# The first two head groups of an mLSTM kernel worked off together instead of one after the other

## The chip, the cores and the metric

The kernel runs on one core of one Trainium2 chip. The metric is the device time in microseconds (us) of one execution, as the median of several runs; "span" is the length of one profiled execution from its first to its last instruction.

## What is computed

Three parts in a row: an mLSTM attention with a running maximum over time, a soft mixture of experts (MoE), and an MLP with a squared ReLU. Shapes: 4 batches, 8 heads, 768 steps, head size 40; 3072 tokens of 320 values behind it. Cut to what matters:

```python
def _attn_ref(q, k, v, i_gate, f_gate, o_gate):
    for t in range(S):                      # S = 768, all B*H = 32 heads at once
        m_new = maximum(f_gate[t] + m, i_gate[t])
        f_stab, i_stab = exp(f_gate[t] + m - m_new), exp(i_gate[t] - m_new)
        m = m_new
        C = f_stab * C + i_stab * einsum('bhd,bhe->bhde', v[t], k[t])
        n = f_stab * n + i_stab * k[t]
        y[t] = sigmoid(o_gate[t]) * (C @ q[t]) / maximum(abs(n @ q[t]), 1.0)

def _moe_ref(x, phi, w1, w2):               # x: tokens from y
    logits = x @ phi                        # 32 slots, softmax over tokens and over slots
    slot_out[e] = relu(slot_input[e] @ w1[e]) @ w2[e]
    return softmax(logits, 1) @ slot_out

def _moe2_ref(x, w_in, w_out):
    r = maximum(x @ w_in, 0.0)
    return (r * r) @ w_out
```

## The kernel before

The 768 steps are cut into NC = 6 chunks of 128 (L), the 32 heads into NG = 11 groups of three (the last has two). A **unit** is one chunk of one group; `units` (L417) lists the 66 units group by group: (0,0), (0,1) ... (0,5), (1,0) and so on. The order of instructions is written out by hand: each engine works off its own instructions in the order of the code, and so does the SyncE queue (SP), which issues all DMAs.

**Gate phases.** `prep(c0, c1)` (L330) turns the gates of all heads into what the units need, for chunks 0-1, 2-3 and 4-5; START (L34) names its steps by a digit for the pair of chunks and a letter: `f` and `m` are the two scans on VectorE (DVE), `i` the subtraction between them, `h` the copy of the maximum to bf16 on ScalarE (ACT), `p` the previous maximum, `a` and `b` subtractions in front of the two exponentials `A` and `B` on ACT, `r`, `u`, `l`, `v` the split of the remainder into bf16 parts (M3), `q` the transposes on TensorE (PE) that make the per-step columns `qt3`. A `G` behind a step puts it on GpSimd (POOL).

**Unit steps.** START uses capitals for the steps of a unit: `M` (e_mb, PE, three matmuls that spread M3), `E` (e_exp, ACT, three exponentials, L451), `K` (e_sel, POOL, causal mask, L458), `T` (e_st, PE, k times q, L468), `P` (e_pm, DVE, product, L480), `W` (e_wv, POOL, weighted v, L424). `D` is one step of `prep_dec` (decay factors `dec120`), `Z` the zeroing of the second group's k buffer on POOL, `~n` are n idle-filling matmuls (L197), `~~n` a second kind (L205).

**Start and loop.** All of START up to the first `|` runs ahead of the loop; each following part runs at the end of one loop pass. Pass i of the loop (L879) issues, for unit i = (g, c): loads for later groups, e_u (L493, the state update, not in the last chunk), T of unit i+2, M of unit i+3, e_uc (L509, L512) and its mask on POOL (e_mask, L528), P of unit i+2, E of unit i+3, in odd passes the products with v of the last two units (e_av, L553), e_inter (L538), K of unit i+3, and in turn the numerators (e_num). The matmul passes of fp32 operands show as two instructions.

**Fillers.** Work of other stages is handed out in small steps by `filler` and `advance`: the tanh of the output gate (sigm, L651), the finish of a group (fin: POOL products L613, DVE L622), the MoE logits of a batch (moe_tokens, L668, L674; each third waits for the groups that it reads), and the narrowing of w_in (win_all, loads at L168, ACT L140 and L144, DVE L148 and L152).

**Buffers.** Group g uses `par[g % 2]` for k (block-diagonal, zeroed once), q, and the token-major v and k; so the loads of group g+2 wait for the last readers of group g.

Of the kernel before, what the change touches and what calls it, by code (L numbers as in the profile page):

```python
# [33 lines left out]
START = "~42 1f 1i 1m 1h 1p 1b 1B 1aG 1r 2f 1u 1A 1v 1q 1l M0 2iG E0 M1 K0 W T0 T1 2m E1 K1 3f 2p 2b 2a ~24 2h 3i 3m 2B Z0 2r 2A 2v 2u P0 3p 3bG D0 3h Z1 ~3 2q ~~5 2l M2 E2 D0 P1 3a 3A 3B K2 D0 D0 3r 3u D0 | 3l 3v 3q | D1 D1 | D1 D1 D1 |"  # L34
# [8 lines left out]
def kernel(  # L43
# [155 lines left out]
    def warm64(n):  # L199
        t = bank("m")  # L200
        for w in (128, 41):
            for _ in range(n):
                for o, r in ((dum, 0), (t, 64)):
                    a = ident[r : r + 40]
                    nc.tensor.matmul(o[:, 0:w], lhsT=a, rhs=a[:, 0:w], start=True, stop=True)  # L205

# [111 lines left out]
    nc.vector.tensor_reduce(out=gmask, in_=gj, axis=AX.X, op=ALU.add)  # L318
    nc.vector.tensor_reduce(out=gs3, in_=gj.rearrange("p g j -> p j g"), axis=AX.X, op=ALU.add)
    nc.vector.tensor_copy(hsel, gs3.unsqueeze(2).to_broadcast([32, 3, D]))  # L320
    nc.vector.tensor_copy(sel4, selF.unsqueeze(1).to_broadcast([128, 4, 32]))
# [523 lines left out]
    def start_exp(c):  # L845
        e_mb(0, c)
        e_exp(0, c)
        e_sel(0, c)
# [30 lines left out]
    for i, (g, c) in enumerate(units):  # L879
        if c == NC - 2 and 0 < g + 2 < NG:  # L880
            load_kb(g + 2)
        if i == 0:
            load_kb(1)
        if c == 0 and g + 1 < NG:
            load_q(g + 1)
        if c == 1 and g + 1 < NG:
            load_kv(g + 1)
        if i == 0:
# [62 lines left out]
        if i in (0, 2):  # L951
            e_wv(0, i + 2, i + 4)
        elif i > 2 and i + 3 < NU and units[i + 3][1] % 3 == 0:
            e_wv(units[i + 3][0], units[i + 3][1], units[i + 3][1] + 3)
# [525 lines left out]
```

## Time and profile before

| | us |
|---|---|
| median of 3 runs | 397.05 (396.72 to 397.13) |
| the profiled execution, whole | 396.4 |
| its span | 394.7 |
| PE busy in the span | 381.7 (97%) |
| DVE / ACT / POOL busy | 264.8 / 251.9 / 103.3 |
| the loop's first e_u starts | 17.39 |

The profiled execution has 1.7 us around its span and lies 0.65 us under the median. Engines run side by side, so busy times do not add up. PE's busy time includes modelled ends of pipelined matmuls, so that a busy PE can still have waited; the chain of work that ended last tells where it did.

### The profile page before, as it was taken

Reading aid. Unit: us, or ns where it says so; the run is one execution under the profiler, and the core shown is the slowest. Engines: PE = TensorE matmul, PEld = TensorE weight load, DVE = VectorE, ACT = ScalarE, POOL = GpSimd, SP = SyncE. Lnnn points to the kernel's source line nnn. Section 1 sums busy time; section 2 is a strip of 40 time slices with the busy share of each in tenths; the row PEclk is TensorE's granted clock in tenths of the full one; section 3 lists DMA queues with packets and bytes.
Section 4 is the critical chain, followed back from the end, with each engine's and each line's share of the span. In section 5 each row is a group of like instructions: output and inputs, shape, how many; then the busy total and the mean of one; then the engine's idle time right before and its main releaser. Section 6 shows DMA issues by size and latency. Waiting matters only on the chain.

```text
span 394.7 us, 9282 instructions
## 1 busy us (share of the span) xinstructions
PE 381.7 (97%) x3497; PEld 337.2 (85%) x3497; DVE 264.8 (67%) x612; ACT 251.9 (64%) x575; POOL 103.3 (26%) x208
## 2 busy tenths in 40 slices
PE   7998999999999999999998999999999999999996
PEld 5888889889888885434688999999999999999996
DVE  8857788887988686546699856555655655655551
ACT  3677665677667752345598776676666667667662
POOL 6565676767667646100000000000000000000000
PEclk9999999999999999999999999999999999999999
DMA  6588578799879789899100020010001002001001
GB/s 203 168 264 281 181 211 275 244 343 351 268 276 315 213 320 321 284 330 424 48 1 2 0 69 1 2 66 2 1 17 51 2 0 68 0 2 67 2 0 66
DMA packets 18665, 56.62 MB, mean 143 GB/s; under 512 B 2357, under 2 KB 6181, under 8 KB 18237
## 3 DMA queue, kind: packets, MB, share of 16 engines
q1 hardware_dynamic: 18621, 56.04, 41.7%
q8 instruction: 27, 0.44, 0.5%
q14 instruction: 17, 0.14, 0.1%
HBM read 52.10 MB, written 3.93 MB: 142 GB/s over the span
## 4 chain that ended last, share of the span: by engine, by line
PE 79%; DMA 5%; ACT 3%; POOL 2%; DVE 2%; issue 2%; SPq 0%; DVEq 0%; ACTq 0%; POOLq 0%
PE ps_mb L1378 17%; PE ps_st L1378 15%; PE ps_lt L1378 8%; PE ps_st L468 8%; PE ps_o L553 5%; PE ps_o L538 4%; PE ps_o L1302 4%; DMA ring<-in_w_dram 3%; PE ps_st L493 3%; PE ps_mb L437 2%; PE ps_m L668 2%; PE ps_m L1302 2%; PE ps_lt L674 2%; DMA stage<-in_w_in_dram 1%; PE ps_st L1098 1%
## 5 line engine op out<-in xcount | busy, mean ns | idle before, releaser
L1325 DVE CAST hi<-ring 128x512 fp32r<-128x512 f32 x91 | 38.8, 426 | 60.7 <-ACT ring L1324 50.7
L1326 DVE TENSOR_TENSOR lo<-ring,hi 128x512 fp32r<-128x512 f32 x96 | 66.5, 693 | 10.0
L451 ACT ACTIVATE w<-ps_mb,qt 128x128 f32<-128x128 f32 x192 | 56.7, 370 | 22.9 <-PE ps_mb L437 18.7
L1307 ACT ACTIVATE ring<-ps_o 128x512 f32<-128x512 f32 x65 | 38.9, 598 | 36.6 <-PE ps_o L1302 36.5
L1324 ACT ACTIVATE ring<-ring 128x512 f32<-128x512 f32 x91 | 57.5, 632 | 2.9
L468 PE MATMUL ps_st<-par 120*128 120x128 f32 (+1 forms) x384 | 54.0, 276 | 0.0
L1378 PE MATMUL ps_mb<-wohlh,hi 128*128 128x320 f32 x160 | 49.6, 311 | 0.0
L1378 PE MATMUL ps_mb<-wohlh,lo 128*128 128x320 f32 x160 | 49.5, 310 | 0.0
L1378 PE MATMUL ps_mb<-wohll,hi 128*128 128x320 f32 x160 | 49.3, 309 | 0.0
L468 PEld LDWEIGHTS ps_st<-par 120*128 120x128 f32 (+1 forms) x384 | 47.9, 191 | 0.5 <-issue 0.5
L458 POOL TENSOR_SCALAR_AFFINE_SELECT w<-w 128x384 f32<-128x384 f32 (+1 forms) x66 | 36.8, 559 | 37.4 <-ACT w L451 28.7
L1378 PE MATMUL ps_st<-wohlh,hi 128*128 128x320 f32 x144 | 44.8, 311 | 0.0
L1378 PE MATMUL ps_st<-wohlh,lo 128*128 128x320 f32 x144 | 44.7, 310 | 0.0
L1378 PE MATMUL ps_st<-wohll,hi 128*128 128x320 f32 x144 | 44.6, 310 | 0.0
L480 DVE TENSOR_TENSOR p<-ps_st,w 128x384 f32<-128x384 f32 (+1 forms) x66 | 35.5, 538 | 4.9 <-POOL w L458 3.8
L1378 PEld LDWEIGHTS ps_mb<-wohll,hi 128*128 128x128 f32 x160 | 30.1, 188 | 1.3
L1307 ACT ACTIVATE ring<-ps_m 128x512 f32<-128x512 f32 x31 | 18.5, 598 | 18.8 <-PE ps_m L1302 18.8
L1378 PEld LDWEIGHTS ps_mb<-wohlh,hi 128*128 128x128 f32 x160 | 30.0, 188 | 0.0
L1378 PEld LDWEIGHTS ps_mb<-wohlh,lo 128*128 128x128 f32 x160 | 30.0, 188 | 0.0
L553 PE MATMUL ps_o<-par,p 128*64 128x41 f32 x768 | 29.0, 232 | 0.0
L1378 PEld LDWEIGHTS ps_st<-wohll,hi 128*128 128x128 f32 x144 | 27.1, 188 | 1.3
L1302 PE MATMUL ps_o<-cst,gst 128*128 128x512 f32 x65 | 26.2, 403 | 2.0 <-ACT gst L1345 2.0
(271 smaller groups left out, 792.0 us busy)
## 6 DMA issues: line engine op xcount, KB each, us to landing
ring<-in_w_dram SPq DMA_DIRECT2D x24, 640.0 KB
stage<-in_w_in_dram SPq DMA_DIRECT2D x10, 512.0 KB
par<-in_w_dram SPq DMA_DIRECT2D x6, 640.0 KB
out_dram<-ring SPq DMA_DIRECT2D x24, 160.0 KB
par<-in_v_s_dram SPq DMA_DIRECT2D x10, 369.0 KB
par<-in_k_s_dram SPq DMA_DIRECT2D x10, 360.0 KB
par<-in_k_t_dram SPq DMA_DIRECT2D x29, 120.0 KB
par<-in_q_t_dram SPq DMA_DIRECT2D x9, 384.0 KB
```

Source lines behind the costliest of these rows:

```text
L451: nc.scalar.activation(w[:, j, :], mb[:, 128 * j : 128 * j + 128], AF.Exp, bias=qt3[:, c, h0 + j : h0 + j + 1])
L458: nc.gpsimd.affine_select(out=w, in_=w, pattern=[[0, nh], [1, 128]], compare_op=ALU.is_ge, fill=0.0, base=0, channel_multiplier=-1)
L468: nc.tensor.matmul(st[:, 128 * j : 128 * j + 128], lhsT=kbd[g % 2][0:nd, j, ts_], rhs=qin[g][0:nd, ts_], start=True, stop=True,)
L480: nc.vector.tensor_tensor(out=p, in0=sts.pop((g, c))[:, 0 : nh * 128].rearrange("p (n t) -> p n t", n=nh), in1=ws.pop((g, c)), op=ALU.mult,)
L538: nc.tensor.matmul(pos[g, c // 2][:, o0 : o0 + nv], lhsT=qin[g][0:nd, 128 * c : 128 * c + 128], rhs=cbds[g, c - 1][0:nd], start=True, stop ...
L553: nc.tensor.matmul(po[t0 : t0 + 64, o0 : o0 + DV], lhsT=p[:, j, t0 : t0 + 64], rhs=vin[g][:, c, j, :], start=True, stop=True,)
L1302: nc.tensor.matmul(t, lhsT=gst[n][:, 128 * k : 128 * k + 128], rhs=cst[tg], start=True, stop=True)
L1307: nc.scalar.activation(r, t, AF.Relu)
L1324: nc.scalar.activation(r, r, AF.Square)
L1325: nc.vector.tensor_copy(hi, r)
L1326: eng.tensor_tensor(out=lo, in0=r, in1=hi.bitcast(F32), op=ALU.subtract)
L1378: nc.tensor.matmul(acc[u][:, 0:DM], lhsT=l_[:, 128 * u : 128 * u + 128], rhs=wohl[r_, f // 8][:, f % 8, :], start=(f == 0 and a == 0), sto ...
```

## The change

Units (0,*) and (1,*) are taken in turn, two chunks of each: (0,0), (0,1), (1,0), (1,1), (0,2), (0,3), (1,2) ... (1,5); from group 2 on the order is as before. So unit 2 is (1,0) and not (0,2). Chunks 2-3 of the gates are first read by unit 4 and chunks 4-5 by unit 8. Phase 3 and `2q` move from the start into the parts behind `|`. The second group's k, q and v are loaded ahead of the loop, its k buffer is zeroed by ACT (three `activation` with scale 0, one of them for the second half of group 0's buffer, in place of a DVE memset). The subtractions `a` and `b` go: `b` becomes a small negation, and `A` and `B` become one exponential per chunk with a bias column. The small selector operations move behind `1v` (`S`) and behind the start. The loads of group 2 come in two parts, at passes 6 and 10. Output-gate tanh starts at pass 4 and w_in at pass 8 (before: 0 and 5).

```diff
-START = "~42 1f 1i 1m 1h 1p 1b 1B 1aG 1r 2f 1u 1A 1v 1q 1l M0 2iG E0 M1 K0 W T0 T1 2m E1 K1 3f 2p 2b 2a ~24 2h 3i 3m 2B Z0 2r 2A 2v 2u P0 3p 3bG D0 3h Z1 ~3 2q ~~5 2l M2 E2 D0 P1 3a 3A 3B K2 D0 D0 3r 3u D0 | 3l 3v 3q | D1 D1 | D1 D1 D1 |"
+START = "~30 1f 1i 1m 1h 1p 1b 1B 1A 1r 1u 1v S 2f 1l T0 T1 1q M0 2i E0 W0 K0 M1 E1 ~16 2m 2h D0 2p 2b K1 W2 2r 2u 2A D0 2v 2B P0 M2 E2 K2 2l D0 P1 D0 ~8 | 2q 3f | 3i 3m 3h D1 | 3p 3b 3B 3A D1 3r 3u 3v | 3l 3q D1 D1 | D2 | D2 | D2 D2 |"
...
-    nc.vector.memset(kbd[0][:, :, 0 : S // 2], 0.0)
-    nc.vector.memset(kbd[0][:, :, S // 2 : S], 0.0)
-    for cs in (slice(0, S // 2), slice(S // 2, S)):
-        load_kb(0, cs)
-        load_q(0, cs)
-    load_kv(0)
+    halves = slice(0, S // 2), slice(S // 2, S)
+    nc.vector.memset(kbd[0][:, :, halves[0]], 0.0)
+    for g, cs in ((1, halves[0]), (0, halves[1]), (1, halves[1])):
+        z = kbd[g][:, :, cs]
+        nc.scalar.activation(z, ident[0 : 3 * D, 0:1].unsqueeze(2).to_broadcast(list(z.shape)), AF.Copy, scale=0.0)
+    for g in range(2):
+        load_kb(g, halves[0])
+        load_q(g, halves[0])
+        load_kv(g)
+    for g in range(2):
+        load_kb(g, halves[1])
+        load_q(g, halves[1])
...
+        def neg():
+            nc.vector.tensor_scalar(
+                out=nlast[32:64, cs], in0=mm[32:64, cs, L - 1 : L], scalar1=-1.0, scalar2=None, op0=ALU.mult
+            )
+        def exp_i():
+            for c in range(c0, c1):
+                t = q3[32:64, c, :]
+                nc.scalar.activation(t, t, AF.Exp, bias=nlast[32:64, c, :])
+        def exp_m():
+            for c in range(c0, c1):
+                nc.scalar.activation(q3[64:96, c, :], mm[64:96, c, :], AF.Exp, scale=-1.0, bias=mprev[64:96, c, :])
...
-            "a": sub(q3[64:96, cs], mprev[64:96, cs].to_broadcast([32, w, L]), mm[64:96, cs]),
-            "b": sub(q3[32:64, cs], q3[32:64, cs], last),
-            "A": exp(64),
-            "B": exp(32),
+            "b": neg,
+            "A": exp_m,
+            "B": exp_i,
...
-    units = [(g, c) for g in range(NG) for c in range(NC)]
+    units = [(g, c0 + c) for c0 in range(0, NC, 2) for g in range(2) for c in range(2)]
+    units += [(g, c) for g in range(2, NG) for c in range(NC)]
...
+        cb = cb01[g, c % 2] if g < 2 else wk.tile([120, nh, DV], F32, tag="cbd", name="cbd", bufs=2)
...
-    pds = [prep_dec(0, 4), prep_dec(4, NC)]
-    begin["W"] = lambda: e_wv(0, 0, 2)
+    pds = [prep_dec(c, c + 2) for c in range(0, NC, 2)]
+    begin["W"] = lambda n: e_wv(units[int(n)][0], 0, 2)
+    begin["S"] = selectors
...
+        if i in (6, 10):
+            cs = (0, 4) if i == 6 else (4, NC)
+            load_kb(2, slice(L * cs[0], L * cs[1]))
+            load_q(2, slice(L * cs[0], L * cs[1]))
+            load_kv(2, *cs)
...
-        if i == 0:
+        if i == 4:
             add(sigm(0), ("sig", 0))
...
-        if i == 5:
+        if i == 8:
             add(win_all(), "win")
...
+        if i + 3 < NU:
+            g3, c3 = units[i + 3]
+            if g3 < 2 and i % 2:
+                e_wv(g3, c3, min(c3 + 2, NC - 1))
+            elif g3 > 1 and c3 % 3 == 0:
+                e_wv(g3, c3, c3 + 3)
```

## Rows read from the trace of the kernel before

**Rows 1.** The page: PE's busy tenths in 40 slices of the span.

```profile
PE   7998999999999999999998999999999999999996
```

**Rows 2.** Chain of work that ended last, in order: start us, length us, engine, line.

```profile
26.23 5.72 DMA stage<-in_w_in_dram
...
37.81 1.10 POOL numr L613 x2
...
53.79 0.48 PE ps_o L538 x2
...
60.09 0.27 PE ps_o L538 x2
...
63.72 0.27 PE ps_o L538 x2
```

**Rows 3.** Timeline of the first 14 us: start us, length us, engine, line, tiles [idle before].

```profile
1.43 6.47 PE L197 MATMUL ps_lt<-ident 128*128 128x256 bf16 x42 [1.43 <-POOL dm L277]
2.09 0.20 ACT L278 ACTIVATE dm<-dm 1x1 f32<-1x1 f32 x1
2.44 1.02 DVE L282 MEMSET par<- 120x1152 f32 x1 [0.31 <-DVE par L281]
...
4.27 0.17 DVE L318 TENSOR_REDUCE ring<-ring 32x11 f32<-32x33 f32 x1
...
4.90 0.67 DVE L349 TENSOR_TENSOR_SCAN ring<-ring 96x256 f32<-96x256 f32 x1
...
6.85 0.42 ACT L377 ACTIVATE M<-ring 96x256 bf16<-96x256 f32 x1 [4.56 <-DVE ring L355]
...
9.92 1.65 ACT L451 ACTIVATE w<-ps_mb,qt 128x128 f32<-128x128 f32 x6
...
11.60 1.91 DVE L365 TENSOR_TENSOR ring<-ring 32x256 f32<-32x256 f32 x3
```

**Rows 4.** Timeline from 14 to 34 us, same columns: the end of the start, the loop's first passes.

```profile
15.79 0.42 DVE L365 TENSOR_TENSOR M<-ring,M 32x256 bf16<-32x256 f32 x1 [0.28 <-ACT M L384]
...
16.36 0.54 DVE L480 TENSOR_TENSOR p<-ps_st,w 128x384 f32<-128x384 f32 x1
...
17.25 0.88 ACT L451 ACTIVATE w<-ps_mb,qt 128x128 f32<-128x128 f32 x3 [0.76 <-PE ps_mb L437]
...
17.39 0.47 PE L493 MATMUL ps_st<-wv,par 128*120 128x123 f32 x2
...
22.23 0.38 PE L493 MATMUL ps_st<-wv,par 128*120 128x123 f32 x2
...
33.18 0.38 PE L493 MATMUL ps_st<-wv,par 128*120 128x123 f32 x2
```

**Rows 5.** Timeline, SP's first DMA issue: start us, length us, what.

```profile
0.81 0.39 SPq L279 DMA_DIRECT2D ring<-in_f_gate_dram  x1
```

**Rows 6.** Bytes moved by stretch: us, length, granted PE clock, DMA share, GB/s.

```profile
2.00:2.50 0.50, 1.00 0.99 338
...
3.50:4.00 0.50, 1.00 0.83 246
```

**Rows 7.** Groups of ACT instructions by line and shape: count, busy us, mean ns, idle before.

```profile
L651 ACT ACTIVATE x<-x 128x640 f32<-128x640 f32 x12 | 9.1, 758 | 0.0
L140 ACT ACTIVATE wi<-stage 128x512 f32<-128x512 f32 x10 | 7.0, 698 | 2.4 <-DMA stage<-in_w_in_dram 2.4
L368 ACT ACTIVATE ring<-ring 32x256 f32<-32x256 f32 x6 | 2.5, 413 | 1.1 <-DVE ring L365 1.0
L386 ACT CAST M<-ring 32x256 bf16<-32x256 f32 x3 | 1.2, 404 | 1.5 <-DVE ring L371 1.4
L346 ACT COPY qt<-ps_o 128x192 f32<-128x192 f32 x3 | 0.9, 309 | 0.1
```

**Rows 8.** Busy time by stretch: PE, PEld, DVE, ACT, POOL (instructions), PE clock, DMA.

```profile
0.00:5.00 5.00, 3.57 (x17) 2.55 (x18) 3.47 (x12) 1.49 (x2) 3.80 (x23) 1.00 0.47 147
...
80.00:100.00 20.00, 19.98 (x266) 17.89 (x266) 16.52 (x42) 15.07 (x45) 14.15 (x26) 1.00 0.99 344
```

More of the change, by code (lines that the diff above doesn't have):

```diff
@@ L197, in warm @@
             nc.tensor.matmul(dum if t is None else t[:, 0:256], lhsT=zb[:, 0:128], rhs=zb, start=True, stop=True)
[L199 to L205, printed above, removed]
     kin, vin, xb = {}, {}, {}
@@ L228, in load_kv @@
             dst[g] = t.rearrange("p (c n d) -> p c n d", c=NC, d=w)
-            nc.sync.dma_start(out=t, in_=src[S * w * h0 : S * w * (h0 + nh)].rearrange("(p f) -> p f", p=128))
+            fs = slice(c0 * nh * w, c1 * nh * w)
+            nc.sync.dma_start(
+                out=t[:, fs], in_=src[S * w * h0 : S * w * (h0 + nh)].rearrange("(p f) -> p f", p=128)[:, fs]
+            )
     def load_x(b, cs):
@@ L317, with selectors @@
     nc.vector.tensor_copy(sel96, selF[0:96])
[L318 to L321, printed above, removed]
+    def selectors():
+        nc.vector.tensor_reduce(out=gmask, in_=gj, axis=AX.X, op=ALU.add)
+        nc.vector.tensor_reduce(out=gs3, in_=gj.rearrange("p g j -> p j g"), axis=AX.X, op=ALU.add)
+        nc.vector.tensor_copy(hsel, gs3.unsqueeze(2).to_broadcast([32, 3, D]))
     def flat(t):
@@ L327 @@
     dec = gt(32, [NC, 1])
+    nlast = gt(96, [NC, 1])
+    cb01 = {(g, p): gt(120, [3, DV]) for g in range(2) for p in range(2)}
     q3, mm, r1 = ig, fg, dl
@@ L338, in prep @@
         tail = mm[:, c0 - 1, L - 1 : L] if c0 else 0.0
-        last = mm[32:64, cs, L - 1 : L].to_broadcast([32, w, L])
-        tt = {"D": nc.vector.tensor_tensor, "G": nc.gpsimd.tensor_tensor}
         def qt():
-            t = bank("o")
+            t = ltb
             for c in range(c0, c1):
@@ L364, in sub @@
         def sub(o_, a, b):
-            return lambda e="D": tt[e](out=o_, in0=a, in1=b, op=ALU.subtract)
-        def exp(r):
-            return lambda: nc.scalar.activation(q3[r : r + 32, cs], q3[r : r + 32, cs], AF.Exp)
+            return lambda: nc.vector.tensor_tensor(out=o_, in0=a, in1=b, op=ALU.subtract)
+        def neg():
+            nc.vector.tensor_scalar(
+                out=nlast[32:64, cs], in0=mm[32:64, cs, L - 1 : L], scalar1=-1.0, scalar2=None, op0=ALU.mult
+            )
+        def exp_i():
[5 more added lines that the diff above has]
+                nc.scalar.activation(q3[64:96, c, :], mm[64:96, c, :], AF.Exp, scale=-1.0, bias=mprev[64:96, c, :])
         def rest():
@@ L843 @@
     w2p = [par[a][:, HS * n : HS * n + HS] for a in (1, 0) for n in range(3)]
[L845 to L848, printed above, removed]
     begin = {"1": prep(0, 2), "2": prep(2, 4), "3": prep(4, NC)}
-    pds = [prep_dec(0, 4), prep_dec(4, NC)]
-    begin["W"] = lambda: e_wv(0, 0, 2)
+    pds = [prep_dec(c, c + 2) for c in range(0, NC, 2)]
+    begin["W"] = lambda n: e_wv(units[int(n)][0], 0, 2)
+    begin["S"] = selectors
     begin["D"] = lambda n: next(pds[int(n)], None)
-    begin["Z"] = lambda h: nc.gpsimd.memset(kbd[1][:, :, S // 2 * int(h) : S // 2 * (int(h) + 1)], 0.0)
     def run(seq):
         for ch in seq.split():
-            if ch[:2] == "~~":
-                warm64(int(ch[2:]))
-            elif ch[0] == "~":
+            if ch[0] == "~":
                 warm(int(ch[1:]))
             elif ch[0] in "MEKTP":
-                {"M": e_mb, "E": e_exp, "K": e_sel, "T": e_st, "P": e_pm}[ch[0]](0, int(ch[1:]))
+                {"M": e_mb, "E": e_exp, "K": e_sel, "T": e_st, "P": e_pm}[ch[0]](*units[int(ch[1:])])
             elif ch[0] in "123":
@@ L870 @@
     run(start.pop(0))
+    nc.vector.tensor_copy(sel4, selF.unsqueeze(1).to_broadcast([128, 4, 32]))
     add(merge(), "merge")
@@ L879 @@
     for i, (g, c) in enumerate(units):
-        if c == NC - 2 and 0 < g + 2 < NG:
-            load_kb(g + 2)
-        if i == 0:
[L883 to L888, printed above, removed]
+        if i in (6, 10):
[3 more added lines that the diff above has]
+            load_kv(2, *cs)
+        if g and c == NC - 2 and g + 2 < NG:
+            load_kb(g + 2)
+        if g > 1 and g + 1 < NG:
+            if c == 0:
+                load_q(g + 1)
+            if c == 1:
+                load_kv(g + 1)
+        if i == 4:
             add(sigm(0), ("sig", 0))
@@ L939 @@
                     add(fin(g1), ("fin", g1), [("sig", b) for b in batches(g1)])
-        elif i > 1 and (c > 1 and g < NG - 1 or c == 1 and g <= GL):
+                nm = None
+        elif i > 1 and nm:
             finish(nm)
-            if c == 1:
-                add(fin(g - 1), ("fin", g - 1), [("sig", b) for b in batches(g - 1)])
+            g1, c1 = units[i - 2]
+            if c1 == NC - 1:
+                add(fin(g1), ("fin", g1), [("sig", b) for b in batches(g1)])
         elif g == NG - 1 and c > 1:
@@ L950 @@
                     next(f1)
[L951 to L954, printed above, removed]
+        if i + 3 < NU:
[4 more added lines that the diff above has]
+                e_wv(g3, c3, c3 + 3)
         if start:
```

3 lines of the change are left out of this document (1 added, 2 removed).

## The prediction

> **What bounds the kernel now.** I read the slices of the page first. PE shows a 9 in nearly every slice; the first ones are the exception [rows 1]. So time can be had where PE still waits, near the beginning, or from PE's own work, which this change hardly touches. The next view is the chain of work that ended last. From 54 us to the end of the loop (about 144 us) it runs over PE instructions alone; two pieces stand for them, the same step of two neighbouring pairs of passes, 3.63 us apart [rows 2]. Ahead of 54 us the chain leaves PE twice: for a w_in load of 5.72 us and for products on POOL [rows 2]. The timeline says where the loop begins: its first e_u runs at 17.39 us, the one of pass 8 at 33.18 [rows 4], and pass 18 begins when the last e_inter of pass 17 starts, at 53.79 [rows 2]. A pair of full passes costs PE 3.63 us when nothing else holds it (one e_u less, about 0.2, where a last chunk is in it).
>
> So there are four stretches: the start (0 to 17.39), passes 0 to 7 (15.8 us for about 14.3 us of PE work), passes 8 to 17 (20.6 us for about 17.7 us of unit work and 1.2 us of MoE fillers), and the rest. The profiled execution is 396.4 us with 394.7 of span, 0.65 under the median of 397.05; I work in differences of its span and take them off the median.
>
> **The rest, first.** I followed the filler list by hand through both orders of units. Before, group 0's finish is handed in at pass 7, group 1's at pass 13; after, at 11 and 13. The first MoE third moves from passes 11 to 13 to passes 14 to 16, and w_in's first loads from pass 5 to 8. From pass 17 on every filler step, every load and every later w_in step falls on the same pass as before. What follows is then the old kernel moved in time, and the change is worth what pass 18 is moved by.
>
> **The start, step by step.** *DVE.* The first scan starts at 4.90, behind two memsets, copies and selector operations. The second memset (1.02) goes, and the selectors, which run from 4.27 to the scan (0.63), move behind it [rows 3]: at most 1.65 us. But the scan needs f_gate, issued at 0.81 [rows 5]. The four half-us stretches from 2.0 to 4.0 move 0.60 MB [rows 6], which is f_gate and i_gate (288 KB each): the one is there by 3 to 3.5, the other by 4 to 4.5. So the gain lies between 0.6 and 1.6; I take 1.2, since i_gate is needed only one scan later.
>
> *ACT.* Three zeroings of 1152 elements stand ahead of the first gate step. The trace has none. ACT takes 0.758 us for 640 elements and 0.698 for 512 [rows 7]; 640 elements plus 512 more at 1.0 to 1.1 ns each give 1.25, and 0.42 for 256 to 0.758 for 640 (0.88 ns each) gives 1.2. From 2.29 [rows 3] they end at about 6.0. Phase 1h, at 6.85 before [rows 3], could start at 5.6 by DVE, so it starts at 6.0: **0.85 us**, not 1.2 (if one zeroing took as long as 1.6 us, nothing). The loads of k wait for zeroings; group 0's first half waits for the DVE memset alone, as before.
>
> The trace shows no zeroing of this size on ACT, and the Trainium skill has a rule for it: ScalarE: Activation LUTs, What ACT_TABLE_LOAD costs, gives 186 ns plus 0.833 ns an element with immediate operands, so an estimate of 1.15 us each and an end at 5.7, 0.3 earlier. Its extra 93 ns for a bias column agrees with the rows, as the exponentials (128 elements, with bias) come at 0.29 apart [rows 4].
>
> *Chain from 1h to the first exponential E0*: 6.85 to 9.92 before [rows 3]. After, on ACT: 1h 0.42 [rows 3], then B and A as two pieces each at 0.29 (a third of 0.88 [rows 4]; two old ones at 0.41 each [rows 7]), u and v 0.40 each [rows 7], then the spread M0 (0.4). That is 2.8 against 3.07; the dropped subtractions ran beside it. **0.25 us.**
>
> *From E0 to the loop*: 7.47 us before, and here lies most. P1 ran at 16.36 behind phase 2 and much of phase 3 in DVE's queue, and E2, with unit 2 in chunk 2, at 17.25, since it needs 2l at 15.79 [rows 4]. After, unit 2 needs phase 1 only, and phase 3 stands behind the loop's first passes. ACT's queue from E0 to E2: E0 and E1 1.7 [rows 3], 2h 0.42, the decay exponential (a few elements, taken at 0.2), 2u and 2v 0.8, 2A and 2B 1.2: 4.3 us, with E0 at 8.8, so E2 at 13.1 to 13.5. DVE beside it: P1 (0.54 [rows 4]) stands behind 2r, P0 and 2l and ends at about 13.2. e_u(0,0) then comes at 13.3, plus 0.3 for hops between engines: 13.6. **The start is 3.8 us shorter** in all (13.1 to 14.8 for e_u, by the bounds above).
>
> What the start gets in return: the second group's loads (1.5 MB) ahead of the loop, issued on SP in front of phi and the gate outputs. Their time is hidden as long as they land before pass 0's T (at 13.6) and W2; by the rate of the four stretches (0.3 MB a us) 3.6 MB are through near 13 us, and the second group's first half, needed first, near 10. Behind W2 on POOL waits K2, which waits for E2 at 13.3 anyway. Before, they were issued behind the start.
>
> **Passes 0 to 7.** 15.8 us before. PE gets 2q in addition (0.4). ACT now has, in these passes: eight E (7.0), phase 3 with 2q's and 3q's copy (0.3 each [rows 7]), 3h, A, B, u, v (3.0 in all), tanh from pass 4 (three at 0.76 [rows 7]) and two numerator copies (taken at 0.25): 12.8 us of at least 14.7. DVE gets some 3.2 us of phase 3 (two scans at 0.67, two subtractions and r at 0.42, small ones) to its eight P at 0.54 and as many e_uc at about 0.3, 11 in all of 14.7. So both fit, with waits in passes 2 to 4, where four ACT phases stand ahead of E6: I take 15.2, **0.6 us less**, with bounds of 14.7 and 18.1 (below).
>
> In the start three DVE subtractions took 1.91 us together [rows 3], 0.64 each, while one alone takes 0.42 [rows 4]; POOL worked beside the three. A rule of the Trainium skill speaks against moving them into the loop, where POOL is busy: SBUF — State Buffer, Who interferes with whom, says that a DVE operation with two SBUF inputs and a reading POOL operation exclude each other for a whole instruction. By the rows' 0.22 each, five such steps (the scans, i, r, l) cost 1.1 us of DVE, inside its slack; by full blocking behind a mask of half a us each it would be some 2.6, an estimate, still inside it.
>
> **Passes 8 to 17.** 20.6 us before, with two waits: ACT stood 2.4 us for w_in [rows 7], issued at 26.23 amid other loads [rows 2], and POOL was late with the finish of group 0 and of group 1. After, w_in is issued behind group 2's first part and its first ACT step comes after E11 and a tanh, so this wait may go (up to 1.5 us). But the two finishes, six products in two at 1.10 [rows 2], now fall on passes 12 to 15 together, beside POOL's masks; that can cost 1 to 2. At pass 14 the numerators need group 0's finish done, so its last DVE steps are pulled in front. I set it at **nothing**, with -1.5 and +1.5. Group 2's loads come in two parts behind the last readers of group 0; they have four passes each until use.
>
> **Sum.** 3.8 + 0.6 + 0.1 (one e_u less ahead of pass 8) + 0 = 4.5 us: 397.05 - 4.5 = 392.5.
>
> **Rivals.** *The start gains, and w_in's wait goes too* (passes 8 to 17 at their PE work, passes 0 to 7 at 14.7): 6.5 us, 390.5. For it: ACT's 2.4 us of idle time had this load as its cause; against it, POOL.
>
> *Startup data or the zeroing come late*: f_gate lands so late that 0.6 remains, or the second group holds T of pass 0. Then the start gains 2 us and the total is 395. Against it: the rate of the first 4 us.
>
> *The gate phases cost in the loop what they took out of the start* (slower). Before, three phases (3l, 3v, 3q) in pass 0 made the first pair 4.84 us long (17.39 to the next pair's 22.23 [rows 4]), 1.2 over 3.63. Fourteen phases stand in passes 0 to 3 now. At 0.4 each they cost 5.6, in place of the 1.5 lost in passes 0 to 7 before, and with the two finishes' 1.5 on POOL the total is -3.9 + 4.1 + 1.5, so 1.7 us slower: 398.7. From 0.3 us a phase on, with POOL as late, the gain is used up. Against it: part of that first pair was 3q's and the decay's own PE work, and the queues have room on average.
>
> *DMA is the bound behind PE*: at 80 to 100 us its share is 0.99 [rows 8]; if loads cannot be drawn ahead, the end stays near 397. Against it: the chain there has no DMA piece, and loads are tied to passes, so they move along. Also PE's clock: the first 17 matmuls took 3.57 us, 210 ns each [rows 8], the 42 of that row 6.47 us [rows 3], so about the last 25 took 116 each: 1.2 and then 2.4 GHz. A fall back in the new gap before T0 would cost some 2 us each time.
>
> **Chances.** Forecast 392.5 (391.0 to 394.0): 0.60. Better (389.5 to 391): 0.13. Late data or partial loss (394 to 396.2): 0.14. DMA or clock takes it all (about 397): 0.06. Slower: 0.07. A measurement tells apart about 0.2%, 0.8 us. So faster 0.87, within it 0.06, slower 0.07. The range that leaves out no more than 2 in 10 is 390.0 to 396.0.
>
> **What would show it.** Right: e_u(0,0) near 13.6, E2 near 13.3, pass 8 near 28.8, the first e_inter of pass 18's chain near 49.3, and 3.63 us a pair behind it. Wrong: a first exponential no earlier than 9.9 (data or zeroing), pairs over 4.5 us in passes 0 to 7 with PE waiting on ACT, POOL the chain's engine in passes 12 to 16, DMA pieces in the chain between 80 and 140 us, or a granted clock below 1.

## The result, and the profile after

The changed kernel takes 401.72 us (median of 4 runs, 400.1 to 403.51) against 396.88 us of the kernel before in the same runs: a ratio of 1.0121, 95% interval 1.0097 to 1.0145. It is **slower by 4.8 us**, where 392.5 was forecast and the range ended at 396.0. The profiled execution took 401.94 us with 400.2 of span, 0.2 over its median, against 396.4 and 394.7 before, so the two traces differ by 5.5 us of span.

The page of the changed kernel, PE's busy tenths in 40 slices as in [rows 1], and below them the granted TensorE clock in tenths of full speed:

```profile
PE   7979799999999999999998999999999999999996
...
PEclk9989979999999999999999999999999999999999
```

Two slices of the clock's row stand out, which in the kernel before holds a 9 everywhere: the third (20 to 30 us) with an 8 and the sixth (50 to 60) with a 7. PE's own row shows the waits (a 7 in the third and the fifth slice) but not the clock: in the sixth slice it holds a 9.

The start ends where it was forecast. Timeline of the changed kernel, the columns of [rows 3]:

```profile
2.20 3.25 ACT L280 ACTIVATE par<-ident 120x1152 f32<-120x1152 f32 x3
...
3.97 0.69 DVE L351 TENSOR_TENSOR_SCAN ring<-ring 96x256 f32<-96x256 f32 x1 [0.37 <-DMA ring<-in_f_gate_dram]
...
6.20 0.42 ACT L390 ACTIVATE M<-ring 96x256 bf16<-96x256 f32 x1 [0.75 <-DVE ring L357]
...
7.62 1.58 PE L481 MATMUL ps_st<-par 120*128 120x128 f32 x12 [1.18 <-DMA par<-in_q_t_dram]
...
9.75 1.66 ACT L464 ACTIVATE w<-ps_mb,qt 128x128 f32<-128x128 f32 x6
...
13.61 0.37 PE L506 MATMUL ps_st<-wv,par 128*120 128x123 f32 x2
...
14.33 1.66 ACT L464 ACTIVATE w<-ps_mb,qt 128x128 f32<-128x128 f32 x6
```

The loop's first e_u is at 13.61 in place of 17.39 [rows 4]. What follows it is read best from busy time by stretch, with the columns of [rows 8]: span of the stretch, then PE, PEld, DVE, ACT and POOL with their instructions, the clock, the DMA share, GB/s. The stretches are passes 0 to 7 and passes 8 to 17, each from one e_u to another. Before:

```profile
17.39:33.18 15.79, 14.96 (x200) 13.78 (x200) 8.54 (x25) 11.30 (x35) 7.07 (x14) 1.00 0.85 272
...
33.18:54.55 21.37, 19.84 (x263) 17.95 (x262) 16.93 (x41) 15.63 (x48) 16.82 (x32) 1.00 0.62 205
```

The changed kernel:

```profile
13.61:33.16 19.55, 17.36 (x207) 15.90 (x206) 12.75 (x39) 13.65 (x46) 8.60 (x19) 0.91 0.51 169
...
33.16:58.88 25.72, 22.93 (x261) 20.49 (x260) 17.62 (x41) 15.38 (x44) 16.01 (x29) 0.87 0.66 214
```

The lead of 3.78 us is gone at pass 8 (33.16 against 33.18), and at pass 18 the kernel is 4.33 behind (58.88 against 54.55). Nearly the same number of matmuls takes PE 2.4 and 3.1 us longer, under a clock of 0.91 and 0.87, and PE stands still longer as well (19.55 - 17.36 = 2.2 against 0.8, and 2.8 against 1.5). The last logits matmul of the tail comes at 162.35 in place of 157.97, 4.38 later: from pass 18 on the old order is only shifted. The last 1.1 us lie behind that; the one piece of the chain there that I found longer is a load, 13.20 us where before has 12.15 for the piece `ring<-in_w_dram`:

```profile
177.11 13.20 DMA ring<-in_w_dram
```

**The first wait, in pass 3.** Timeline of the changed kernel; PE's transposes of phase 3 (`3q`, L347) wait for ACT's second exponential (`3A`, L381), and this for the steps of phase 3 in DVE's queue:

```profile
16.32 0.80 DVE L351 TENSOR_TENSOR_SCAN ring<-ring 96x256 f32<-96x256 f32 x1
...
18.60 1.06 DVE L357 TENSOR_TENSOR_SCAN ring<-ring 96x256 f32<-96x256 f32 x1
...
19.69 0.42 ACT L390 ACTIVATE M<-ring 96x256 bf16<-96x256 f32 x1 [2.28 <-DVE ring L405]
...
20.10 0.84 ACT L464 ACTIVATE w<-ps_mb,qt 128x128 f32<-128x128 f32 x3
...
21.12 0.29 DVE L585 TENSOR_TENSOR tmp<-ps_o,qt 128x123 f32<-128x123 f32 x1 [0.76 <-ACT num L584]
...
21.57 0.16 DVE L370 TENSOR_SCALAR ring<-ring 32x2 f32<-32x2 f32 x1
...
21.76 0.69 ACT L377 ACTIVATE ring<-ring 32x128 f32<-32x128 f32 x2 [0.67 <-DVE ring L370]
...
22.46 0.69 ACT L381 ACTIVATE ring<-ring 32x128 f32<-32x128 f32 x2
...
22.91 0.59 PE L347 MATMUL ps_lt<-ident,ring 96*128 96x96 f32 x2 [2.19 <-ACT ring L381]
...
23.75 0.47 PE L506 MATMUL ps_st<-wv,par 128*120 128x123 f32 x2
```

The delay passes through three queues. The second scan ends at 19.66; ACT has stood idle for 2.28 us in front of `3h` (L390), which reads its result (the row names the small DVE step behind the scan as the releaser), and pass 2's three exponentials E (L464) stand behind `3h` in ACT's queue. A numerator step on DVE (L585) waits 0.76 us for an ACT copy behind these exponentials, and the negation `3b` (L370), which `3B` needs, stands behind that step.

At pass 3 (18.21 against 23.97 before) the lead was 5.8 us. `3q` is first needed for unit 8, whose E is issued in pass 5, but PE works off its instructions in order: pass 4's e_u stands behind it and comes at 23.75.

**The second wait, in pass 14.** Same view; here two releasers follow each other, POOL and DVE:

```profile
45.11 1.13 POOL L626 TENSOR_TENSOR numr<-num,rc 128x240 f32<-128x240 f32 x2
...
46.20 0.56 POOL L541 TENSOR_TENSOR cbd<-cu,hm 120x123 f32<-120x123 f32 x1
...
46.81 0.48 PE L551 MATMUL ps_o<-cbd,par 120*128 120x123 f32 x2 [1.30 <-POOL cbd L541]
...
47.74 1.10 DVE L635 SCALAR_TENSOR_TENSOR x<-x,numr 128x240 f32<-128x240 f32 x2
...
48.38 0.43 PE L681 MATMUL ps_m<-ident,x 128*120 128x128 f32 x2 [0.87 <-DVE x L635]
...
48.65 0.37 PE L506 MATMUL ps_st<-wv,par 128*120 128x123 f32 x2
```

Two products of group 0's finish stand on POOL ahead of the mask that e_inter needs; then the finish's last DVE steps stand ahead of the MoE transposes (L681), which the program issues in the same pass. Pass 14 takes 4.36 us (44.29 to 48.65), in the kernel before 1.42 (46.77 to 48.19).

**The clock.** Busy time by stretch of the changed kernel; the clock is the third number from the end:

```profile
24.00:25.00 1.00, 1.00 (x12) 0.99 (x12) 0.10 (x1) 0.98 (x4) 0.10 (x1) 1.00 0.00 0
25.00:26.00 1.00, 1.00 (x8) 1.00 (x7) 0.60 (x2) 0.90 (x4) 1.00 (x3) 0.56 0.00 0
26.00:28.00 2.00, 2.00 (x21) 1.74 (x21) 1.60 (x6) 1.28 (x5) 1.17 (x3) 0.50 0.06 12
...
45.00:49.00 4.00, 1.83 (x17) 1.41 (x16) 3.15 (x8) 1.65 (x7) 4.00 (x9) 1.00 0.49 186
49.00:53.00 4.00, 4.00 (x39) 3.66 (x38) 3.27 (x8) 1.33 (x4) 4.00 (x7) 0.50 0.51 154
53.00:56.00 3.00, 3.00 (x20) 2.51 (x19) 1.06 (x4) 1.76 (x6) 0.90 (x2) 0.53 0.98 243
```

After each wait the granted clock falls from 1.00 to 0.50 (2.4 to 1.2 GHz): from about 25 to 28.5 us and from about 49 to 55.8 us. PE had been idle for 2.19 us in one piece before the first fall, and busy for only 1.83 of 4 us before the second. Both falls come a little after PE is at work again, so the loss shows in busy time. Both stretches of before shown above stand at 1.00.

### The profile page after: what moved, and what is told of

The parts are those of the page before. It is cut to its first block, busy times and chain, and to the rows that moved or that the text cites. A ratio compares the mean times of both kernels' runs of the same rounds, so it can differ in the third digit from the quotient of the medians.

```text
span 400.2 us, 9193 instructions
## 1 busy us (share of the span) xinstructions
PE 383.6 (96%) x3444; PEld 337.9 (84%) x3444; DVE 264.0 (66%) x614; ACT 256.7 (64%) x585; POOL 99.7 (25%) x204
## 4 chain that ended last, share of the span: by engine, by line
PE 80%; DMA 5%; ACT 4%; DVE 4%; issue 3%; POOL 2%; SPq 1%; POOLq 0%; DVEq 0%; ACTq 0%
PE ps_mb L1393 16%; PE ps_st L1393 15%; PE ps_st L481 9%; PE ps_lt L1393 8%; PE ps_o L566 5%; PE ps_o L551 4%; PE ps_o L1317 4%; DMA ring<-in_w_dram 3%; PE ps_st L506 3%; PE ps_mb L450 2%; PE ps_m L681 2%; PE ps_lt L687 2%; PE ps_m L1317 2%; DMA stage<-in_w_in_dram 1%; ACT w L464 1%
## 5 line engine op out<-in xcount | busy, mean ns | idle before, releaser
L464 ACT ACTIVATE w<-ps_mb,qt 128x128 f32<-128x128 f32 x192 | 56.5, 368 | 23.4 <-PE ps_mb L450 19.4
L481 PE MATMUL ps_st<-par 120*128 120x128 f32 (+1 forms) x384 | 55.9, 283 | 1.2 <-DMA par<-in_q_t_dram 1.2
L481 PEld LDWEIGHTS ps_st<-par 120*128 120x128 f32 (+1 forms) x384 | 49.7, 197 | 2.4 <-DVE ring L322 1.4
L1393 PE MATMUL ps_st<-wohll,hi 128*128 128x320 f32 x144 | 44.6, 310 | 0.0
L566 PE MATMUL ps_o<-par,p 128*64 128x41 f32 x768 | 30.1, 236 | 0.0
L566 PEld LDWEIGHTS ps_o<-par,p 128*64 128x64 f32 x768 | 26.2, 143 | 3.7 <-issue 0.6
```

Source lines behind the costliest of these rows:

```text
L464: nc.scalar.activation(w[:, j, :], mb[:, 128 * j : 128 * j + 128], AF.Exp, bias=qt3[:, c, h0 + j : h0 + j + 1])
L481: nc.tensor.matmul(st[:, 128 * j : 128 * j + 128], lhsT=kbd[g % 2][0:nd, j, ts_], rhs=qin[g][0:nd, ts_], start=True, stop=True,)
L566: nc.tensor.matmul(po[t0 : t0 + 64, o0 : o0 + DV], lhsT=p[:, j, t0 : t0 + 64], rhs=vin[g][:, c, j, :], start=True, stop=True,)
L1393: nc.tensor.matmul(acc[u][:, 0:DM], lhsT=l_[:, 128 * u : 128 * u + 128], rhs=wohl[r_, f // 8][:, f % 8, :], start=(f == 0 and a == 0), sto ...
```

## The experiments

Every kernel starts from the changed one. In each group all were timed beside the kernel before, whose median was 396.74, 396.71 and 396.52 us in the three groups. The changed kernel itself was not timed again in them: a difference from its 401.72 us leans on the kernel before, whose medians lie within 0.4 us of each other. Of START, a diff shows only the piece that changes. **My theory** after reading the traces: two PE waits, each made dearer by the clock. The **rivals**: that the waits are caused elsewhere (two finishes at once; ACT being full), or that the clock is a side show and the waits alone count.

### First group: which wait, and is the clock a cause?

**e1** moves `3q` to the end of the next pass, behind two decay steps (`D1`):

```diff
-| 3l 3q D1 D1 | D2 |
+| 3l D1 D1 | 3q D2 |
```

> The changed kernel with step 3q (transposes of the gate columns) issued at the end of pass 4 instead of pass 3. Theory 'waits on the gates, then the clock': in the changed kernel PE stood from 20.72 to 22.91 us in front of 3q, and its granted clock was 0.5 from about 25.1 to 28.5 us, so the 5.8 us that pass 3 was early were gone at pass 8 (33.16 against 33.18). Without 3q in front, PE waits at most for the decay factors (about 1.2 us), the clock stays at 1, pass 8 begins 2.5 to 4 us earlier, and as the second gap (45 to 49 us) stays, the time falls by 2 to 4 us to about 398 to 399.5. Rival 'the time is lost in loads and in the tail' (the w2 loads took 13.2 us of the chain against 12.15): within 1 us of the changed kernel, about 401.

Measured: 396.55 us (395.3 to 399.15, 10 runs), ratio 0.9992 (0.9970 to 1.0014). One step moved gives back 5.2 us, more than the 2 to 4 expected: the second wait stays, as expected, but in this profile the clock does not fall behind it. PE's busy time by stretch:

```profile
13.64:30.85 17.21, 15.55 (x207) 14.38 (x205) 12.69 (x39) 13.27 (x46) 8.17 (x19) 1.00 0.58 192
...
30.85:53.96 23.11, 19.98 (x260) 17.75 (x259) 17.04 (x41) 15.36 (x44) 16.13 (x29) 1.00 0.70 232
```

The same 207 and 260 matmuls take 15.55 and 19.98 us, against 17.36 and 22.93 in the changed kernel: 1.8 and 2.95 us are the price of the clock. The waits have not all gone; the same kernel's timeline:

```profile
21.99 0.38 PE L417 MATMUL ps_m<-ring 32*120 32x22 f32 x2 [1.25 <-DVE ring L409]
...
45.00 0.48 PE L551 MATMUL ps_o<-cbd,par 120*128 120x123 f32 x2 [1.28 <-POOL cbd L541]
...
46.57 0.43 PE L681 MATMUL ps_m<-ident,x 128*120 128x128 f32 x2 [0.87 <-DVE x L635]
```

In pass 3 the decay's matmul now waits 1.25, and pass 14 still takes 4.34 us (42.50 to 46.84), but at full clock. So one and the same wait in pass 14 is followed by a fall in one profile and not in the other.

**e2** leaves the wait and fills it with 19 idle-filling matmuls ahead of `3q`:

```diff
-| 3l 3q D1 D1 |
+| 3l ~19 3q D1 D1 |
```

> The changed kernel with 19 idle-filling matmuls in front of 3q, where PE waits 2.2 us anyway (19 at 0.115 us are 2.2 us). The wait for the gates stays, only PE is busy in it. If the lower clock behind the gap is what costs, the stretch at 0.5 from 25 to 28.5 us goes and the time falls by about 1.7 us, to some 400. If the clock is a bystander and the wait itself costs, the time stays (401.7). If the idle-filling matmuls delay 3q, it rises by up to 0.5.

Measured: 397.55 us (395.66 to 400.26, 10 runs), ratio 1.0033 (1.0006 to 1.0060), 4.2 us under the changed kernel although pass 4 begins at 23.70, as there (23.75). The first fall is gone, and pass 8 comes at 31.55. That is more than the 1.7 us expected. In this profile the second fall is still there (0.50 from 49 to 53 us), but the profiled run (399.65 us, mean clock 0.991) is one of the three longest of ten: those took 399.6 to 400.3 us at a mean clock of 0.990 or 0.991, the other seven 395.7 to 398.3 at 0.995 or more. The changed kernel's four runs all lie at 0.982 to 0.990. So with the first fall gone the second came in some runs only; why is open.

**e3** hands in the finish of group 1 at pass 16 in place of 13, so that the two finishes do not meet:

```diff
-            if c1 == NC - 1:
+            if c1 == NC - 1 and g1 != 1:
                 add(fin(g1), ("fin", g1), ...)
...
+        if i == 16:
+            add(fin(1), ("fin", 1), ...)
```

> The changed kernel with the finish of group 1 handed in at pass 16 instead of 13, so that the two finishes (six products of about 0.57 us on POOL, six operations of about 0.65 us on DVE) no longer stand together in passes 12 to 16. Theory 'POOL and DVE crowd, then the clock': PE waited 1.3 us for POOL and 0.9 for DVE between 45.3 and 48.7 us, and its clock was 0.5 from 49.0 to 55.8 us, so passes 14 to 18 took 14.3 us against 7.4 before. With the finishes apart, that stretch shrinks by 3 to 6 us: 396 to 399. Rival 'loads': no change, about 401.7. Rival 'the forced finish of group 0 at pass 14 is the cause, not the two together': the gap stays and the time is within 1 us.

Measured: 404.1 us (402.58 to 405.76, 4 runs), ratio 1.0205 (1.0170 to 1.0240): slower still. Pass 14 takes 4.17 us. **The theory that the two finishes crowd each other there falls**: group 0's alone makes the wait. The loop does end earlier (the last logits at 159.78, not 162.35), but in this profile the clock stood at 1.00 behind pass 14, which is worth about as much. And the shift of a filler moves w_in's last load by a slot, and two loads of the tail with it. SP's queue in e3, and the chain of work that ended last:

```profile
130.31 0.35 SPq L168 DMA_DIRECT2D stage<-in_w_in_dram  x1
...
159.60 1.02 SPq L123 DMA_DIRECT2D stage<-in_w_dram  x2
```

```profile
164.48 11.15 DMA xTw<-in_w_out_dram
```

In the tail this costs twice: PE is busy for 44.6 of the 50 us from 150 us on (47.2 in the changed kernel), and the granted clock falls once more (0.72 from 175 to 180 us; 1.00 in the changed kernel). SP's queue in the changed kernel, where the two `stage` loads go out 13.8 us earlier:

```profile
145.76 1.14 SPq L123 DMA_DIRECT2D stage<-in_w_dram  x2
```

**e4** is e1 and e3 together (both diffs above).

> Both: 3q at the end of pass 4 and the finish of group 1 at pass 16. If the two gaps are the loss and independent, the gains add up: 393 to 396, so faster than the kernel before (396.9). If the second gap only takes up what the first one leaves (the same limit hit later), the sum is no better than the better one of the two.

Measured: 401.82 us (401.14 to 406.35, 4 runs), ratio 1.0158 (1.0098 to 1.0218), 2.3 under e3 and 5.3 over e1. Its `stage` loads go out at 158.99, so the price of the late loads in the tail is there again (a clock of 0.69 from 175 to 180 us); the finish stays at pass 13 from here on. In its profile the clock is also at 0.50 from 24 to 25 us, behind a wait in pass 3 of 1.27 us, where e1's was 1.25.

### Second group: the price of the clock alone, and pass 14

**e6** removes no wait; it fills both:

```diff
+| 3l ~19 3q D1 D1 |
...
+        if i == 14:
+            warm(11)
         e_inter(g, c)
+        if i == 14:
+            warm(8)
```

> The changed kernel with idle-filling matmuls in both gaps: 19 in front of 3q, and in pass 14 eleven in front of e_inter and eight behind it. No wait is taken away; PE is only busy while it waits. If the lower clock is the greater part of the loss, no stretch at 0.5 is left and the time is 396 to 397, 5 us under the changed kernel, with runs close together (within 1 us). If the waits are, it stays above 399.

Measured: 396.5 us (395.83 to 397.83, 12 runs), ratio 0.9991 (0.9971 to 1.0010). Passes 3 and 14 are as long as in the changed kernel (18.16 to 23.68, and 43.68 to 48.04, 4.36), and the time is 5.2 us less. Busy time by stretch of e6, where the changed kernel shows 0.56, 0.50, 0.50 and 0.53:

```profile
25.00:26.00 1.00, 1.00 (x11) 0.99 (x11) 0.64 (x2) 0.96 (x4) 1.00 (x3) 1.00 0.06 16
26.00:28.00 2.00, 2.00 (x37) 1.85 (x35) 1.75 (x7) 1.28 (x5) 1.14 (x3) 1.00 0.01 4
...
49.00:53.00 4.00, 4.00 (x55) 3.31 (x54) 3.92 (x10) 3.03 (x9) 4.00 (x7) 1.00 0.62 183
53.00:56.00 3.00, 3.00 (x46) 2.84 (x45) 2.55 (x6) 1.74 (x5) 1.58 (x3) 1.00 0.96 287
```

This is the test that tells the theory from its last rival: with both waits whole and the clock kept, the loss is gone, to within the interval (1.2 us faster to 0.4 slower than the kernel before). **The clock accounts for the 4.8 us by which the kernel was slower; the waits, with 0.7 us more of PE's own work, took most of the start's gain.** The runs agree more closely too (2.0 us from end to end, 3.9 in e1).

**e5** is e1 with the first MoE third of batch 0 held until pass 15, behind the finish's DVE steps:

```diff
+        if kt == 0 and not b:
+            need.add("go")
...
+        if i == 15:
+            done.add("go")
```

> 3q at the end of pass 4, and the first MoE transposes held back until pass 15. In every kernel with the new order so far PE loses about 2.2 us in pass 14: it waits 1.3 us for POOL (the mask of the state behind two products of group 0's finish) and then 0.9 us with two of four transposes issued, for DVE's last steps of that finish, which are pulled into the same pass. With the transposes a pass later only the first wait is left. Theory 'the wait in pass 14 is the transposes behind the finish': pass 15 begins 0.8 to 1 us earlier than with 3q moved alone (46.84), the clock has less of a gap to fall in, 395 to 395.8. Theory 'POOL alone': pass 15 stays within 0.3 us, 396.5.

Measured: 395.96 us (394.8 to 397.5, 12 runs), ratio 0.9972 (0.9951 to 0.9994). Pass 14 takes 2.85 us; the wait for L635 is gone, the one for POOL stays, as the timeline of e5 shows:

```profile
44.36 0.48 PE L551 MATMUL ps_o<-cbd,par 120*128 120x123 f32 x2 [1.31 <-POOL cbd L541]
...
49.36 0.46 PE L551 MATMUL ps_o<-cbd,par 120*128 120x123 f32 x2 [0.73 <-DVE num L592]
```

**e7** is e1 with the decay steps of chunks 2-3 (`D1`) spread over passes 0 to 3, each ahead of phase 3's steps:

```diff
-| 2q 3f | 3i 3m 3h D1 | 3p 3b 3B 3A D1 3r 3u 3v | 3l D1 D1 | 3q D2 |
+| 2q D1 3f | D1 3i 3m 3h | D1 3p 3b 3B 3A 3r 3u 3v | D1 3l | 3q D2 |
```

> 3q at the end of pass 4, and the decay steps of chunks 2-3 spread over passes 0 to 3 (each one pass earlier), so that PE's matmul for them does not stand behind pass 2's gate steps on DVE. With 3q moved alone PE still waited in pass 3, and pass 4 began at 22.30. Theory 'PE stands behind whatever gate step is put into its queue': pass 4 begins at 21 to 21.4, and the time falls by 1 us against 3q moved alone, to 395 to 395.8. Rival 'behind it PE waits for the next thing anyway (the bank of the masks, ACT's E)': pass 4 is earlier, pass 8 is not (30.85), no change in time, 396.5.

Measured: 396.55 us (395.01 to 399.26, 12 runs), ratio 0.9995 (0.9968 to 1.0023), no gain over e1. Pass 4 begins at 21.04 (22.30 in e1), but pass 5 at 23.79 (23.89): the next reader on PE waits 1.07 for the decay's copy in DVE's queue, and pass 8 begins at 30.93 (30.85), as the rival has it. Moving one step has only moved the wait. That DVE's work as a whole sets it in these passes is my reading; no run shows it.

**e8** is e7 with e5's hold.

> 3q at the end of pass 4, the decay steps early and the MoE transposes held until pass 15. If both gaps were waits of PE behind one instruction each, the gains add: 394 to 395, faster than the kernel before (396.7) by 0.5%. If something else is next in both places (POOL in pass 14, ACT in passes 4 to 7), it is within 0.5 us of 3q moved alone, 396 to 396.6.

Measured: 395.88 us (395.04 to 396.86, 12 runs), ratio 0.9969 (0.9950 to 0.9987): e5 again (395.96), and no more from the decay's place.

### Third group: what is left

**e9** is e5 with the tanh of batch 1 from pass 13 on, to see whether ACT delays POOL's mask in pass 14:

```diff
-                late.append((i + SG, b))
+                late.append((i + SG if b > 1 else 13, b))
```

> 3q at the end of pass 4, MoE transposes held until pass 15, and the tanh of the second batch's output gate (three of 0.75 us on ACT) from pass 13 on instead of pass 8. In passes 8 to 11 ACT had four E, three tanh, four w_in pieces and a wait of 0.8 to 1.4 us for w_in, 9 to 10 us of work against 7 us of PE's, so E was late, POOL waited for E (1.0 us) and then had its products of the finish in front of the mask that PE waits for in pass 14 (1.3 us). Theory 'ACT is what is late': pass 14 begins 0.5 to 1 us earlier than 41.83 and the wait for POOL shrinks under 0.6; 395 to 395.5. Theory 'POOL's own products are too many': the wait of 1.3 us stays, 396.

Measured: 396.19 us (394.5 to 397.92, 12 runs), ratio 0.9973 (0.9950 to 0.9995), and PE's wait for POOL in pass 14 is 1.30, as in e5. The tanh on ACT is not its cause.

**e10** is e5 with both remaining waits filled, 10 matmuls ahead of `D1` and 11 ahead of e_inter in pass 14:

```diff
+| 3l ~10 D1 D1 | 3q D2 |
...
+        if i == 14:
+            warm(11)
         e_inter(g, c)
```

> 3q at the end of pass 4, MoE transposes held until pass 15, and idle-filling matmuls in what is left of the two gaps: ten in front of the decay matmul in pass 3 (PE waits 1.2 us there), eleven in front of e_inter in pass 14 (1.3 us). Every kernel of the new order without them shows runs up to 3 us apart. Theory 'the rest of the spread is the clock, falling in some runs': runs within 1 us of each other and a median of 395 to 395.5. Theory 'the spread is from loads': the spread stays at 2 to 3 us and the median at 396.

Measured: 395.2 us (394.25 to 396.12, 12 runs), ratio 0.9953 (0.9931 to 0.9976): 0.8 under e5, though the two intervals overlap, and 1.9 us from end to end in place of 2.7 (not the 1 us expected).

**e11** is e5 with the gates' transposes ahead of the first T, which waits for q:

```diff
-1l T0 T1 1q M0 2i E0 W0 K0 M1 E1 ~16 2m
+1l ~12 1q M0 M1 T0 T1 2i E0 W0 K0 E1 ~4 2m
```

> 3q at the end of pass 4, MoE transposes held until pass 15, and in the start 1q, M0 and M1 in front of T0 and T1, with twelve idle-filling matmuls while PE waits. In the changed kernel T0 waited for q until 7.62 us, 1q behind it ran at 9.03 though its input was there at 8.05, and E0 came at 9.75 where 8.8 was forecast. Theory 'one load in PE's queue holds the gates': E0 near 9.1, first e_u near 13.0 (13.56 without), and the lead holds to pass 8 (30.1 to 30.5 against 30.77); 395.5. Rival 'phase 2 on ACT and DVE sets the loop's begin, not E0': e_u within 0.2 us, no change (396).

Measured: 395.54 us (394.99 to 396.56, 12 runs), ratio 0.9963 (0.9942 to 0.9984). The timeline of e11 has the first M behind the subtraction `1l` and no longer behind q, but the first exponential hardly earlier than 9.75:

```profile
6.56 0.42 ACT L390 ACTIVATE M<-ring 96x256 bf16<-96x256 f32 x1 [1.11 <-DVE ring L357]
...
9.21 0.51 PE L450 MATMUL ps_mb<-M,sel 96*128 96x128 bf16 x6 [0.44 <-DVE M L367]
...
9.65 1.65 ACT L464 ACTIVATE w<-ps_mb,qt 128x128 f32<-128x128 f32 x6 [0.18 <-PE ps_mb L450]
```

The first e_u is at 13.50, 0.1 earlier. That looks like the rival, but the gates themselves were late in this profile: `1h` starts at 6.56 where the changed kernel has 6.20, since i_gate landed later (the subtraction behind it starts at 5.25, not 4.89). The profiles side by side tell what holds what. In the eleven kernels with T0 first, E0 starts 2.13 us behind T0, which waits for q, whether `1h` starts at 6.17 or at 6.66; in e11 and e12 it starts 3.09 behind `1h`. And the first e_u follows E0 by 3.85 to 3.87 us in all thirteen. So q did hold the start, by 0.46 us in the changed kernel's profile (an estimate: 6.20 + 3.09 = 9.29 against 9.75), and E0 sets the loop's begin.

**e12** is e9, e10 and e11 together.

> All of these together: 3q later, MoE held, tanh later, filled gaps, gates first. If each is worth what its theory says, 393.5 to 394.5, 0.6 to 0.8% under the kernel before. If PE's own work of passes 0 to 18 is the floor by now, or a later resource takes the lead away, 395 to 395.8, no better than the best of the three.

Measured: **394.99 us (393.97 to 395.88, 11 runs), ratio 0.9944 (0.9919 to 0.9969)**, the lowest median (e10's interval overlaps) and faster than both kernels. The first e_u is at 13.27, pass 8 at 30.48 (before: 33.18), pass 18 at 53.82 (before: 54.55): of a lead of 4.1 us, 2.7 are left at pass 8 and 0.7 at pass 18; the spans of the two profiles differ by 1.1 (393.6 and 394.7).

## Why the prediction was wrong

**The start (3.8 us earlier): right in its number**, with e_u at 13.61 for 13.6. Inside it the terms moved. The scan came at 3.97, 0.93 earlier for 1.2, held by f_gate as said; 1h at 6.20 for 6.0; the first exponential at 9.75 for 8.8, with half of it from T0's wait for q (e11); E2 at 14.33 for 13.3. I had worked e_u out from E2, but in the trace it comes before E2: it follows a decay matmul (12.41) and idle-filling ones in PE's queue, and the decay's product stands on DVE behind `2r`, which needs `2h`, which stands behind E0 and E1 on ACT. That is 3.86 us behind E0, where I had 4.8. The two misses cancel, so the number of e_u held by luck. The price of the zeroing was nearer to the lower value: three in 3.25 us, 1.05 each from start to start, where the rows gave 1.20 to 1.25. The Trainium skill (ScalarE: Activation LUTs, What ACT_TABLE_LOAD costs) gave an estimate of 1.15; the trace's group of these instructions has a mean of 1.144 us, so the Trainium skill agrees. The 0.29 us that the prediction sets beside it is a distance between starts; one such exponential lasts 0.37 us (the mean of L451 before), as they overlap.

**Passes 0 to 7 (forecast 15.2, bounds 14.7 and 18.1; measured 19.55): the step that failed first.** Three terms. PE's own work was taken as 14.3, by 3.63 a pair; it is 14.96 before and 15.55 after at full clock (e1), 0.6 more than before. The waits were allowed some 0.5 us (15.2 over the bound of 14.7, in passes 2 to 4) and are 2.2, in one piece in pass 3. The prediction summed DVE's and ACT's work against the whole stretch and found that "both fit"; but the steps of phase 3 are a chain across DVE's and ACT's queues that is issued in four passes (0 to 3), with unit steps in between that wait for each other, and its last link stands in PE's queue ahead of work that does not need it. A sum over a stretch cannot show that. The third term, 1.8 us, is the clock, which the sum left out. One small term had the wrong sign: the 0.1 of the sum is for "one e_u less ahead of pass 8", but passes 0 to 7 now have eight e_u in place of seven (no last chunk falls there), and passes 8 to 17 one less.

**Passes 8 to 17 (forecast as before, which between these marks is 21.37, with 1.5 either way; measured 25.72): failed by the clock.** The reason named, group 0's finish pulled in front at pass 14 beside POOL's masks, is the one that the trace shows, and its price lay inside the bound: PE's waits are 2.8 in place of 1.5, 1.3 more. The w_in wait did shrink, from 2.4 [rows 7] to 0.83 us on ACT, and pass 12 was 2.3 us ahead (40.28 against 42.55). What the bounds had no room for is 2.95 us of half clock.

**From pass 18 on: right in the order** (4.33 behind at pass 18, 4.38 at the tail's logits), but 1.1 us were lost behind it to which I have no cause that a run shows. The same stretch, from the tail's last logits matmul to the end of the span, took 236.7 us before, 237.85 after and 236.3 to 237.5 in e1, e5, e6, e9, e10, e11 and e12, so it varies from profile to profile.

The account, at pass 18: start -3.78; passes 0 to 7 waits +1.36, clock +1.81, work +0.59; passes 8 to 17 waits +1.26, clock +2.95, work +0.14; sum +4.33.

**The rivals.** The slower one (gate phases cost in the loop what they saved, 398.7) had the right place, passes 0 to 3, and the right companion, POOL's finish. Its price by phase was not the mechanism: most of what PE paid was for one phase that stood in its queue too early. The clock was in the prediction with "some 2 us each time", close to the 1.8 and 2.95 measured; but I looked for it in the start alone, gave it 0.06 together with DMA, and did not ask whether the waits that I allowed in passes 2 to 4 and at pass 14 would bring it on. That chance was the mis-sized term that decided the sign. Even the reading behind it was loose: I took 1.2 GHz from the 210 ns of the first matmuls, while the granted clock of that row is 1.00 [rows 8], and no run here shows why the two differ at the start. Two of the signs that the prediction named for being wrong did come, a pair over 4.5 us with PE waiting on ACT (passes 2 and 3: 17.16 to 23.75) and a granted clock below 1. The DMA rival did not come: no kernel's chain holds a load between 80 and 140 us.

**DVE beside POOL.** The rule weighed in the prediction (the Trainium skill, SBUF — State Buffer, Who interferes with whom) would have a two-input DVE operation wait out a reading POOL operation. In the trace the second scan of phase 3 took 1.06 us at 18.60, beside a product of 0.60 on POOL (18.51 to 19.11), against 0.69 in the start: 0.37 longer, inside the loss that the prediction allowed. The trace agrees in direction; five such steps at that price are under the slack of the stretch, but three of them (the two scans and the subtraction between) lie in the chain ahead of `3q`.

**What stays open.** What decides whether the clock falls behind a given wait: pass 14's two waits of the same length brought it in the profiles of the changed kernel, e2 and e7 and not in that of e1, pass 3's shorter one in those of e4 and e11 and not in those of e1 and e5, and runs of one kernel without filled waits differ by up to 5.2 us (e4). And of the 4.5 us forecast, e12 gives 1.5: its passes 0 to 7 take 17.2 us with the wait in pass 3 filled but not shortened, and in its passes 8 to 17 PE still stands for 2.2 us in waits of 0.4 to 0.7 for DVE, POOL and ACT, which I did not try to take out.

## What to carry to other kernels

When work is moved off a start into a loop, follow each moved chain to the queue in which its last link stands, and ask what stands behind it there that does not need it; a stretch whose sums fit can still stall. Where PE must wait, as here for 1.25 to 2.2 us, price the wait twice, once as itself and once with the clock halved for some us behind it (3.4 and 6.8 here), and put idle matmuls into it or issue the waiting step a pass later. A filler that is shifted to mend one place also shifts the loads tied to its end, so look at what they release (in e3 two loads went out 13.8 us later, and a load became the chain of the tail for 11.15 us).

## What the runs showed of the hardware

PE waits of 2.2 us in one piece, and of 1.30 and 0.87 close to each other with few matmuls around them, were followed by 3.4 and 6.8 us at 1.2 GHz, though PE was at work again when the clock fell. Matmuls that compute nothing, put into the waits, kept the clock at 2.4 GHz and were worth 5.2 us of 402 without shortening a single wait. With e1's shorter waits (1.25, 1.28 and 0.87 us) the fall came in some runs only: its mean granted clock was 0.999 in a run of 395.3 us and 0.991 in one of 399.15. The kernel before is not free of lower clocks either: four of its runs beside the experiments took 399.75 to 400.65 us at a mean clock of 0.991, where its median was 396.5 to 396.7. Of the 35 runs of the three kernels with both waits filled (e6, e10, e12) none has a mean clock below 0.998 or takes over 397.83 us.
